# Output products of a fused attention and maxout kernel by Strassen's algorithm: seven block products for eight

## The chip, the cores and the metric

The kernel runs on one core of one Trainium2 chip. The metric is the device time of one execution in microseconds (us), the median of several runs. The engines are called as in the profile: PE (TensorE, matmuls; PEld is its weight load), DVE (VectorE), ACT (ScalarE), POOL (GpSimd) and SP (SyncE); a "q" behind a name means the engine's own instruction queue issuing a DMA.

## The reference

The first half is attention with blocks sorted by a soft permutation. `P` comes from five rounds of exp and row and column normalisation of `sort_net`. The second half is a feed-forward layer with a maximum of two hidden projections:

```python
k_sorted = np.einsum('bhij,bhjcd->bhicd', P, k_b)      # 8 blocks of 96 tokens
v_sorted = np.einsum('bhij,bhjcd->bhicd', P, v_b)
attn = softmax(scale * q_b @ k_sb.T)                   # inside each block
x = (attn @ v_sb)  ->  [B*S, H*D] = [3072, 512]
h1 = x @ w1                                            # w1, w2: [512, 1024]
h2 = x @ w2
g = np.maximum(h1, h2)
out = g @ w_out                                        # w_out: [1024, 512]
```

There are 4 batches of 8 heads, 768 tokens and 64 channels. Inputs and output are float32; the kernel computes its matmuls in bf16 with float32 accumulation.

## The kernel before

**The hidden layer.** max(h1, h2) is relu(h1 - h2) + h2, so the kernel keeps w1 - w2 in place of w1 (`w_difference`), computes one hidden product per token and takes its relu as `g`. What is left of h2 goes to the output through `wc` = w2 @ w_out, which `w_product` computes once. An output tile is therefore 12 matmuls with 128 rows of depth each: eight with `g` as the stationary operand and `wo_sb` moving, four with the attention output `xT` and `wc`.

**Tiles.** A batch of 768 tokens is cut into two halves `ch` of 384 (`TCH`) for the hidden layer. `moe_h(b, ch, t)` (lines 670 and 685) makes two of eight blocks of 128 hidden channels for one half in 8 matmuls of 384 columns, and ACT or DVE evicts them with the relu as a tile `g` of 128x768 bf16. The output is made in six token tiles `ti` of 128 tokens and 512 columns: `moe_out` (714) gives each tile 12 matmuls of 512 columns in two parts of six, two tiles share one PSUM tile of 1024 columns (two banks), and one copy evicts both, followed by one store of 512 KB from SP. Tiles 4 and 5 of the last batch go through `moe_out_last` (729), which evicts them one by one and splits the last tile into 384 and 128 columns.

**PSUM.** One pool of four buffers of 1024 float32 columns (line 62) serves everything. A new tile waits until the last reader of its buffer is done.

**Attention.** `sort_k` and the `sort_v` functions mix the blocks by P, `scores` (539) makes one unit of eight score blocks, ACT takes its exp into one of eight buffers `e` (line 555), `values` (567) multiplies by v and DVE evicts the result in two instructions, a reciprocal (586) and a scaled copy (592) into `x`. `x_transposes` (600) turns `x` into `xT`, by PE for batch 0 and by a DMA transpose on SP for the others. `turn_v` (line 250) reorders v on DVE, `pair_q` (407) packs q for batches 2 and 3, and `q_transposes` transposes it, by a DMA on SP in those batches.

**Order.** The schedule is written by hand: instructions stand on each engine in the order of the calls. The first part (about 38 us) loads, normalises P and does the attention and the hidden products of batch 0 by a list of steps. Then a loop over batches runs a list of units: eight `moe_h` (none in batch 0, which has four `w_product` instead), then twelve parts of output tiles. Behind a unit stand steps of the next batch's attention, as three tables (`first_tail`, `second_tail`, `third_tail`, lines 859 to 913) say; the last batch has none. So in batches 0 to 2 the output products alternate with sorts, scores and values of the next batch, and in batch 3 they follow one another. Which of ACT and DVE evicts a tile is decided at build time by `pick` (running sums of estimated work, `load`), or by a letter given.

**Queues.** Loads are issued by POOL, stores and DMA transposes by SP in the order of the calls.

Of the kernel before, what the change touches and what calls it, by code (L numbers as in the profile page):

```python
# [10 lines left out]
FP32 = mybir.dt.float32  # L11
# [5 lines left out]
def kernel(  # L17
# [16 lines left out]
    nc = tc.nc  # L34
# [18 lines left out]
    NE = 8  # L53
# [349 lines left out]
    def pair_q(b, two):  # L403

        if two == 0:
            q_pair[b] = qpool.tile([128, HP, R, 2 * D], BF16, tag="q_pair", name="q_pair", bufs=1)
        nc.vector.tensor_copy(
            out=q_pair[b][:, :, :, two * D : (two + 1) * D],
            in_=q_raw[b][:, two * HP : (two + 1) * HP].rearrange("p h (r d) -> p h r d", r=R),
        )  # L410
        load["D"] += 900
# [125 lines left out]
    e_tiles, x_tiles = {}, {}  # L537

    def scores(b, u, n=0):
# [15 lines left out]
        e = e_bufs[(b * 8 + u) % NE]  # L555
# [142 lines left out]
    out_ps = {}  # L698

    def out_products(dst, b, ti, n0=0, n1=512, part=None):  # L700
        ch, off = divmod(ti * 128, TCH)
        for m in range(NFB + HP) if part is None else range(part * 6, part * 6 + 6):
            hp = m - NFB
            nc.tensor.matmul(  # L704
                dst,
                g_tiles[b, ch, m // 2][:, m % 2, off : off + 128]
                if m < NFB
                else xT[:, b % 2, ch, hp % 2, hp // 2, off : off + 128],
                wo_sb[:, m, n0:n1] if m < NFB else wc[:, hp, n0:n1],
                start=(m == 0),  # L710
                stop=(m == NFB + HP - 1),
            )

    def moe_out(b, ti, part):
        slot = ti % 2
        if slot == 0 and part == 0:
            out_ps[0] = ps_f32("out_ps")
        ps = out_ps[0]
        out_products(ps[:, slot * 512 : (slot + 1) * 512], b, ti, part=part)
        if slot == 1 and part == 1:  # L720
            tok0 = b * S + ti * 128
            o = opool.tile([128, 2, 512], FP32, tag="o", name="o")
            evac(o.rearrange("p t n -> p (t n)"), ps, 1024)
            nc.sync.dma_start(
                out=out[tok0 - 128 : tok0 + 128, :].rearrange("(t p) n -> p t n", p=128),
                in_=o,
            )

    def moe_out_last(ti, pieces):

        tok0 = (B - 1) * S + ti * 128
        for n0, n1, eng in pieces:
            ps = ps_f32("out_ps")
            out_products(ps[:, 0 : n1 - n0], B - 1, ti, n0, n1)
            o = opool.tile([128, n1 - n0], FP32, tag=f"o{ti}{n0}", name="o", bufs=1)
            if eng == "A":
                nc.scalar.copy(out=o, in_=ps[:, 0 : n1 - n0])
            else:
                nc.vector.tensor_copy(out=o, in_=ps[:, 0 : n1 - n0])  # L739
            (nc.scalar if eng == "A" else nc.sync).dma_start(  # L740
                out=out[tok0 : tok0 + 128, n0:n1], in_=o
            )

# [107 lines left out]
    def sorts_and_scores(b):  # L851
# [6 lines left out]
    TURN = [lambda c=c: turn(both, c) for c in (0, 24, 48, 72)]  # L858
    first_tail = {
        7: KS,  # L860
        9: [TQ[0], TURN[0]],
        10: [SC[0], TQ[1], TURN[1]],
        11: SC[1:4] + TURN[2:4] + [lambda half=half: load_v(3, half=half) for half in range(2)],
        12: VS[0:3],
        13: VS[3:6],
        14: VS[6:8] + [SC[4]],
# [5 lines left out]
        20: [VA[4]],  # L872
        21: [VA[5], TR[2]],
        22: [VA[6], VA[7], TR[3]],
# [20 lines left out]
        17: [lambda: pair_q(3, 0)],  # L895
        18: [lambda: pair_q(3, 1)],
# [17 lines left out]
    tails = [first_tail, second_tail, third_tail, {}]  # L914
    for b in range(B):
# [52 lines left out]
```

## Time and profile before

| | us |
|---|---|
| median of the runs (165.81 to 166.31) | 165.84 |
| span of the profiled execution, first to last instruction | 165.0 |
| difference: what lies around the span | 0.84 |
| first output product of batch 0 | 49.8 |
| hidden products of batch 1, 2, 3 begin | 70.9, 104.1, 135.8 |
| output products of batch 1, 2, 3 begin | 84.9, 117.3, 146.2 |
| last output product begins its last four matmuls | 161.5 |

The profiled execution's own device time is not listed apart; its span and the median of the runs stand for it. The page gives each engine's busy time, a row of digits for 40 slices of the span, the chain of work that ended last, and groups of equal instructions with count, busy time, mean duration and the idle time ahead of them. A matmul's listed duration holds its way through the array (380 ns for 512 columns), while matmuls start every 216 ns; the distance between starts is what counts. In the answers on single stretches of time the first column is the start in us from the beginning of the span and the second the length.

### The profile page before, as it was taken

Reading aid. Unit: us, or ns where it says so; the run is one execution under the profiler, and the core shown is the slowest. Engines: PE = TensorE matmul, PEld = TensorE weight load, DVE = VectorE, ACT = ScalarE, POOL = GpSimd, SP = SyncE. Lnnn points to the kernel's source line nnn. Section 1 sums busy time; section 2 is a strip of 40 time slices with the busy share of each in tenths; the row PEclk is TensorE's granted clock in tenths of the full one; section 3 lists DMA queues with packets and bytes.
Section 4 is the critical chain, followed back from the end, with each engine's and each line's share of the span. In section 5 each row is a group of like instructions: output and inputs, shape, how many; then the busy total and the mean of one; then the engine's idle time right before and its main releaser. Section 6 shows DMA issues by size and latency. Waiting matters only on the chain.

```text
span 165.0 us, 4561 instructions
## 1 busy us (share of the span) xinstructions
PE 157.0 (95%) x2007; PEld 95.4 (58%) x2025; DVE 77.5 (47%) x170; ACT 82.3 (50%) x101; POOL 33.9 (21%) x61
## 2 busy tenths in 40 slices
PE   7889999999999999999999999999999999999992
PEld 7839776756554555557655554575655546654451
DVE  4878995684366564525277763250642420000011
ACT  3489776617239846055652353457447206642020
POOL 7949997131206000000014010000000000000000
PEclk9999999999999999999999999999999999999999
DMA  3999999999999999689515999995025294000333
GB/s 41 204 204 194 164 196 207 209 205 220 210 203 204 220 224 167 175 84 228 111 19 104 126 212 157 200 309 29 0 52 175 50 164 142 0 0 0 127 131 127
DMA packets 30404, 23.90 MB, mean 145 GB/s; under 512 B 16752, under 2 KB 25200, under 8 KB 30384
## 3 DMA queue, kind: packets, MB, share of 16 engines
q0 software_dynamic: 11040, 13.37, 50.0%
q1 hardware_dynamic: 19200, 10.17, 28.9%
q8 instruction: 16, 0.26, 0.7%
q10 hardware_dynamic: 144, 0.07, 0.1%
q14 instruction: 4, 0.03, 0.1%
HBM read 26.75 MB, written 6.29 MB: 200 GB/s over the span
## 4 chain that ended last, share of the span: by engine, by line
PE 81%; DMA 6%; DVE 5%; ACT 3%; POOL 2%; issue 2%
PE out_ps L704 37%; PE h_ps L677 25%; DMA w_sb<-in_moe_w_dram 5%; PE wc_ps L657 4%; PE o_ps L575 4%; PE k_ps L458 3%; PE s_ps L548 3%; ACT e L556 1%; POOL w_sb L189 1%; PE v_ps L523 1%; DMA p_sb<-in_sort_net_dram 1%; PE tq_ps L433 1%; DVE colsum L276 1%; DVE p_sb L273 1%; PE tw_ps L638 1%
## 5 line engine op out<-in xcount | busy, mean ns | idle before, releaser
L704 PE MATMUL out_ps<-wo_sb,g 128*128 128x512 bf16 (+2 forms) x187 | 46.0, 370 | 1.4 <-issue 1.0
L677 PE MATMUL h_ps<-xT,w_sb 128*128 128x384 bf16 x256 | 44.5, 326 | 0.0
L677 PEld LDWEIGHTS <-w_sb 128*128 128x128 bf16 x256 | 24.0, 98 | 15.5
L556 ACT ACTIVATE e<-s_ps 96x768 bf16<-96x768 f32 x32 | 24.0, 805 | 14.8 <-PE s_ps L548 14.8
L691 ACT ACTIVATE g<-h_ps 128x768 bf16<-128x768 f32 x27 | 21.7, 811 | 17.4 <-PE h_ps L677 17.3
L704 PEld LDWEIGHTS <-g 128*128 128x128 bf16 x200 | 17.1, 97 | 15.8
L704 PE MATMUL out_ps<-wc,xT 128*128 128x512 bf16 (+2 forms) x98 | 24.7, 370 | 0.1
L108 ACT COPY o<-out_ps 128x1024 f32<-128x1024 f32 x10 | 10.1, 1012 | 28.0 <-PE out_ps L704 25.2
L592 DVE TENSOR_TENSOR x<-o_ps,rs 96x512 bf16<-96x512 f32 x32 | 22.0, 687 | 1.1
L704 PEld LDWEIGHTS <-xT 128*128 128x128 bf16 x100 | 9.6, 97 | 11.2
L575 PEld LDWEIGHTS <-e 96*128 96x128 bf16 x256 | 11.7, 97 | 5.7 <-DVE v_sb L110 0.2
L586 DVE RECIPROCAL rs<-o_ps 96x8 f32<-96x8 f32 x32 | 6.4, 201 | 17.2 <-PE o_ps L575 17.1
L739 DVE COPY o<-out_ps 128x512 f32<-128x512 f32 (+1 forms) x2 | 1.2, 625 | 27.6 <-PE out_ps L704 27.6
L575 PE MATMUL o_ps<-v_sb,e 96*128 96x65 bf16 x256 | 12.7, 193 | 0.0
L110 DVE CAST kT<-k_ps 128x1024 bf16<-128x1024 f32 x6 | 7.2, 1222 | 8.4 <-PE k_ps L458 8.4
L110 DVE CAST v_sb<-v_ps 96x1024 bf16<-96x1024 f32 x7 | 8.5, 1219 | 4.9 <-PE v_ps L523 2.2
L160 POOL DMA_DIRECT2D v_raw<-in_k_dram x3 | 2.5, 838 | 35.1 <-DVE v_dc L250 31.4
L108 ACT CAST v_sb<-v_ps 96x1024 bf16<-96x1024 f32 x9 | 8.8, 1015 | 1.6 <-PE v_ps L500 0.8
L169 POOL DMA_DIRECT2D v_raw<-in_v_dram x11 | 6.5, 593 | 12.7 <-DVE v_dc L250 6.4
L693 DVE TENSOR_SCALAR g<-h_ps 128x768 bf16<-128x768 f32 x5 | 4.8, 957 | 8.9 <-PE h_ps L677 8.8
L548 PEld LDWEIGHTS <-kT 64*128 64x128 bf16 x256 | 6.1, 94 | 4.8 <-issue 2.6
L548 PE MATMUL s_ps<-qT,kT 64*128 64x96 bf16 x256 | 8.5, 204 | 0.3 <-DVE qT L110 0.2
(97 smaller groups left out, 144.4 us busy)
## 6 DMA issues: line engine op xcount, KB each, us to landing
out_dram<-o SPq DMA_DIRECT2D x11, 512.0 KB, 3.4
v_raw<-in_v_dram POOLq DMA_DIRECT2D x8, 384.0 KB, 13.5
k_raw<-in_k_dram POOLq DMA_DIRECT2D x9, 256.0 KB, 11.0
w_sb<-in_moe_w_dram POOLq DMA_DIRECT2D x4, 256.0 KB, 6.0
w_sb<-in_moe_w_dram POOLq DMA_DIRECT2D x2, 512.0 KB, 9.6
wo_sb<-in_moe_w_out_dram POOLq DMA_DIRECT2D x2, 512.0 KB, 13.7
v_raw<-in_v_dram POOLq DMA_DIRECT2D x3, 256.0 KB, 5.0
q_raw<-in_q_dram POOLq DMA_DIRECT2D x4, 192.0 KB, 9.1
```

The lines of the kernel that those rows point to most:

```text
L108: nc.scalar.copy(out=out_ap, in_=in_ap)
L110: nc.vector.tensor_copy(out=out_ap, in_=in_ap)
L169: nc.gpsimd.dma_start(out=v_raw[r0 : r0 + 64, m * n : (m + 1) * n], in_=v_src[b, :, m * n : (m + 1) * n],)
L548: nc.tensor.matmul(ps[:, h2 * 512 + ii * 128 : h2 * 512 + ii * 128 + BLK], kT[b][rows, (hp * 8 + i) * BLK : (hp * 8 + i) * BLK + 128], rhs ...
L556: nc.scalar.activation(out=e[:, 0 : 8 * BLK].rearrange("p (t c r) -> p t c r", t=8, r=R), in_=ps[0:BLK] .rearrange("p (t f) -> p t f", t=8 ...
L575: nc.tensor.matmul(ps[:, h2 * 512 + ii * 65 : h2 * 512 + (ii + 1) * 65], e[:, (h2 * 4 + ii) * BLK : (h2 * 4 + ii) * BLK + 128], v_sb[:, m0 ...
L586: nc.vector.reciprocal(out=rs, in_=ov[:, :, :, 64])
L592: nc.vector.tensor_tensor(out=x, in0=ov[:, :, :, 0:D], in1=rs.to_broadcast([BLK, 2, 4, D]), op=ALU.mult,)
L657: nc.tensor.matmul(ps[:, 0:512], w2T[:, fb, dmt * 128 : (dmt + 1) * 128], wo_sb[:, fb, :], start=(fb == 0), stop=(fb == NFB - 1),)
L677: nc.tensor.matmul(h_ps[ch, t][:, m * 512 : m * 512 + TCH], w1_sb[:, hp, fb * 128 : (fb + 1) * 128], xT[:, b % 2, ch, hp % 2, hp // 2, :], ...
L691: nc.scalar.activation(out=g, in_=src, func=AF.Relu)
L704: nc.tensor.matmul(dst, g_tiles[b, ch, m // 2][:, m % 2, off : off + 128] if m < NFB else xT[:, b % 2, ch, hp % 2, hp // 2, off : off + 12 ...
```

## The change

A batch's output is [768 tokens, 512 columns] = A @ B with a depth of 12 blocks of 128 (eight of `g`, four of `xT`). It is now cut in two along each of the three dimensions: token half `ch` 0 or 1, depth half, and column half of 256 (`NW`). The four block products of each output half, eight together, are replaced by seven products by Strassen's algorithm (in Winograd's form). A token tile of half 0 goes together with that of half 1; there are three such pairs in a batch, two handled as one group (`pair`, 12 matmuls of 256 columns a product) and one alone (`single`, six). A batch has 126 matmuls of 256 columns instead of 72 of 512.

- **Weight sums** (`weight_sums`): T1 to T4 of `wo_sb` and of `wc`, once, on DVE in the tail of batch 0. Six of them take the place of `w2T`, which is no longer needed then.
- **Token sums** (`x_sums`, `g_sums`): S1 to S4 of `xT` (four instructions of 128x768 bf16 a batch; on DVE for batch 0, on POOL for the others, behind the first hidden product) and of `g` (eight a batch, on DVE behind the last hidden product; S3 overwrites its operand).
- **Groups** (`Group.step`): seven products go by turns into the two banks of one PSUM tile; four of the seven accumulate on an earlier product that stays there. After each product one instruction evicts: an ACT copy after products 0 and 2, a DVE add of PSUM and an SBUF tile after the other five. Each group stores twice from SP, 512 KB for the pair and 256 KB for the single tile.
- **The last batch** uses the same groups; `moe_out_last` is gone.
- **Memory**: six `e` buffers instead of eight, and `q_pair` shares the buffer of `q_raw`.
- **Units**: twelve output parts become seven steps of the pair and four units of two, two, two and one steps of the single group; the tails are moved accordingly.

```diff
-    NE = 8
+    NE = 6
+    NW = DMODEL // 2
...
-            q_pair[b] = qpool.tile([128, HP, R, 2 * D], BF16, tag="q_pair", name="q_pair", bufs=1)
+            q_pair[b] = qpool.tile([128, HP, R, 2 * D], BF16, tag="q_raw", name="q_pair", bufs=1)
...
-        e = e_bufs[(b * 8 + u) % NE]
+        e = e_bufs[e_next[0] % NE]
+        e_next[0] += 1
...
-    def moe_out(b, ti, part):
-        slot = ti % 2
-        if slot == 0 and part == 0:
-            out_ps[0] = ps_f32("out_ps")
-        ps = out_ps[0]
-        out_products(ps[:, slot * 512 : (slot + 1) * 512], b, ti, part=part)
-        if slot == 1 and part == 1:
...
-            evac(o.rearrange("p t n -> p (t n)"), ps, 1024)
...
+    def weight_sums(c, which):
+
+        b11, b12, b21, b22 = weight_blocks(c)
+        t1, t3 = (wt_c[:, 0], wt_c[:, 2]) if c else (wt_early[:, 0], wt_early[:, 1])
+        t2, t4 = (wt_c[:, 1], wt_c[:, 3]) if c else (wt_late[:, 0], wt_late[:, 1])
+        out, in0, in1 = {
+            1: (t1, b12, b11),
+            2: (t2, b22, t1),
+            3: (t3, b22, b12),
+            4: (t4, b21, t2),
+        }[which]
+        nc.vector.tensor_tensor(out=out, in0=in0, in1=in1, op=ALU.subtract)
+        load["D"] += 330 if c else 600
+
+    def x_sums(b, which, eng):
+
+        a11, a12, a21, a22 = [xT[:, b % 2, ch, :, half, :] for ch in range(2) for half in range(2)]
+        s1, s2, s3, s4 = [sums_x[:, n] for n in range(4)]
+        out, in0, in1, op = {
+            1: (s1, a21, a22, ALU.add),
+            2: (s2, s1, a11, ALU.subtract),
+            3: (s3, a11, a21, ALU.subtract),
+            4: (s4, a12, s2, ALU.subtract),
+        }[which]
+        eng.tensor_tensor(out=out, in0=in0, in1=in1, op=op)
+
+    def g_sums(b, t):
+
+        a11, a12, a21, a22 = [g_tiles[b, ch, t + 2 * half] for ch in range(2) for half in range(2)]
+        s1, s2, s4 = [sums_g[:, n, t * 2 : t * 2 + 2] for n in range(3)]
+        for out, in0, in1, op in [
+            (s1, a21, a22, ALU.add),
+            (s2, s1, a11, ALU.subtract),
+            (s4, a12, s2, ALU.subtract),
+            (a21, a11, a21, ALU.subtract),
+        ]:
+            nc.vector.tensor_tensor(out=out, in0=in0, in1=in1, op=op)
+        load["D"] += 1900
...
+    class Group:
...
+        def product(self, bank, lw, rw, new):
+            n = 0
+            last = len(self.ks) * len(self.tiles) - 1
+            for k in self.ks:
+                for p, ti in enumerate(self.tiles):
+                    nc.tensor.matmul(
+                        self.ps[:, bank * 512 + p * NW : bank * 512 + (p + 1) * NW],
+                        left(self.b, lw, k, ti * 128),
+                        right(rw, k),
+                        start=new and n == 0,
+                        stop=n == last,
+                        skip_group_check=True,
+                    )
+                    n += 1
...
+        def add(self, ch, half, n, other):
+            nc.vector.tensor_tensor(
+                out=self.part(ch, half), in0=self.by_tile(self.bank(n)), in1=other, op=ALU.add
+            )
+            load["D"] += (60 + self.w) / 0.96
...
+        def step(self):
+            at, self.at = self.at, self.at + 1
+            if at == 0:
+                n = len(self.tiles)
+                self.ps = ps_f32("out_ps")
...
+                self.product(0, "a11", "b11", True)
+                nc.scalar.copy(out=self.a, in_=self.bank(0))
+                load["A"] += (200 + self.w) / 1.2
+            elif at == 1:
+                self.product(1, 2, 2, True)
+                self.add(1, 0, 1, self.by_tile(self.a))
+            elif at == 2:
+                self.product(0, "a12", "b21", False)
+                nc.scalar.copy(out=self.part(0, 0), in_=self.by_tile(self.bank(0)))
+                load["A"] += (200 + self.w) / 1.2
+            elif at == 3:
+                self.product(1, 1, 1, False)
+                self.add(0, 1, 1, self.by_tile(self.a))
+            elif at == 4:
+                self.product(0, 3, 3, True)
+                self.add(1, 1, 0, self.part(0, 1))
+            elif at == 5:
+                self.product(1, 4, "b22", False)
+                self.add(0, 1, 1, self.by_tile(self.a))
+                self.store(0)
             else:
+                self.product(0, "a22", 4, False)
+                self.add(1, 0, 0, self.part(1, 0))
+                self.store(1)
...
     first_tail = {
-        7: KS,
-        9: [TQ[0], TURN[0]],
-        10: [SC[0], TQ[1], TURN[1]],
-        11: SC[1:4] + TURN[2:4] + [lambda half=half: load_v(3, half=half) for half in range(2)],
+        7: KS + XS,
+        8: [GS[0]],
+        9: [TQ[0], TURN[0], WS[0, 1], WS[0, 3]],
+        10: [SC[0], TQ[1], TURN[1], GS[1]],
+        11: SC[1:4]
+        + TURN[2:4]
+        + [WS[0, 2], WS[1, 1], WS[1, 2]]
+        + [lambda half=half: load_v(3, half=half) for half in range(2)],
         12: VS[0:3],
         13: VS[3:6],
-        14: VS[6:8] + [SC[4]],
+        14: VS[6:8] + [SC[4], WS[1, 3], WS[0, 4], WS[1, 4]],
...
-        20: [VA[4]],
-        21: [VA[5], TR[2]],
-        22: [VA[6], VA[7], TR[3]],
+        20: [VA[4], VA[5], TR[2]],
+        21: [VA[6], VA[7], TR[3]],
...
+    def last_h(b):
+        moe_h(b, 1, 3, "A")
+        g_sums(b, 0)
+        g_sums(b, 1)
...
+        pair, single = Group(b, (0, 1), b > 0), Group(b, (2,), b > 0)
+        units += [pair.step] * 7
+        cost += [13] * 7
+        units += [lambda n=n: [single.step() for _ in range(n)] for n in (2, 2, 2, 1)]
+        cost += [13] * 4
         for n, unit in enumerate(units):
-            elapse(100 * cost[n] if n < len(cost) else 0)
+            elapse(100 * cost[n])
             unit()
+            if b > 0 and n == 0:
+                for which in (1, 2, 3, 4):
+                    x_sums(b, which, nc.gpsimd)
```

## The prediction

> **What bounds the kernel now.** I read the page's busy shares and slices first, then the chain by engine and line, the groups by shape for durations, the timeline of the last output tile, and the busy time by stage.
>
> ```profile
> PE 157.0 (95%) x2007; PEld 95.4 (58%) x2025; DVE 77.5 (47%) x170; ACT 82.3 (50%) x101; POOL 33.9 (21%) x61
> PE   7889999999999999999999999999999999999992
> PEclk9999999999999999999999999999999999999999
> PE 81%; DMA 6%; DVE 5%; ACT 3%; POOL 2%; issue 2%
> L704 PE MATMUL out_ps<-wo_sb,g 128*128 128x512 bf16 (+2 forms) x187 | 46.0, 370 | 1.4 <-issue 1.0
> ```
>
> TensorE is busy from 5 us to the end, holds 81% of the chain, and idles 1.4 us before the output products of line 704. Whatever makes it wait is paid in full. The last tile gives rates and latencies:
>
> ```profile
> 159.13 1.46 PE L704 MATMUL out_ps<-wo_sb,g 128*128 128x384 bf16 x8
> 159.34 0.69 DVE L739 COPY o<-out_ps 128x512 f32<-128x512 f32 x1 [26.31 <-PE out_ps L704]
> 160.43 0.81 PE L704 MATMUL out_ps<-wc,xT 128*128 128x384 bf16 x4
> 161.08 0.61 PE L704 MATMUL out_ps<-wo_sb,g 128*128 128x128 bf16 x8
> 161.53 0.39 PE L704 MATMUL out_ps<-wc,xT 128*128 128x128 bf16 x4
> ```
>
> Starts give the rate: eight 384-column matmuls take 160.43 - 159.13, 162 ns each; eight of 128 columns take 0.45 us, 56 ns each, a weight load apiece. So weight loads don't limit even there. Tile 4 left TensorE at 159.13 and its eviction began at 159.34: 0.21 us from the last matmul slot to an eviction.
>
> ```profile
> L739 DVE COPY o<-out_ps 128x512 f32<-128x512 f32 x1 | 0.7, 692 | 26.3 <-PE out_ps L704 26.3
> L330 DVE TENSOR_TENSOR pm<-pe,maskJ 128x320 f32<-128x320 f32 x1 | 0.5, 492 | 0.7 <-PE pe L322 0.7
> L108 ACT CAST wc<-wc_ps 128x512 bf16<-128x512 f32 x3 | 1.8, 586 | 5.8 <-PE wc_ps L657 5.8
> L737 ACT COPY o<-out_ps 128x128 f32<-128x128 f32 x1 | 0.3, 267 | 4.2 <-PE out_ps L704 4.2
> L231 DVE TENSOR_TENSOR w_sb<-w_sb 128x1024 bf16<-128x1024 bf16 x2 | 1.3, 688 | 0.3 <-DMA w_sb<-in_moe_w_dram 0.3
> L231 POOL TENSOR_TENSOR w_sb<-w_sb 128x1024 bf16<-128x1024 bf16 x2 | 4.3, 2146 | 0.4 <-DMA w_sb<-in_moe_w_dram 0.4
> ```
>
> These price the new operations. The busy time of the four output stages (batch 0 to 3) tells what lies beside them:
>
> ```profile
> 49.79:70.94 21.15, 20.49 (x291) 11.43 (x296) 12.47 (x23) 11.73 (x14) 2.18 (x4) 1.00 1.00 197
> 84.63:104.14 19.51, 18.98 (x222) 10.22 (x224) 12.63 (x21) 6.45 (x8) 3.07 (x4) 1.00 1.01 143
> 117.08:135.78 18.70, 18.48 (x174) 9.64 (x176) 6.68 (x15) 7.25 (x9) 0.00 (x0) 1.00 0.45 97
> 146.18:165.00 18.82, 15.63 (x84) 7.71 (x83) 1.25 (x2) 3.10 (x4) 0.00 (x0) 0.99 0.23 84
> ```
>
> Columns: window, length, then busy time of PE, weight load, DVE, ACT, POOL, clock, DMA share, GB/s. Batch 3 has almost nothing but products.
>
> **The change, part by part.** *Products.* A 512-column matmul takes 0.2158 us (the row of twelve from 148.77 to 151.36 in the timeline). With 56 ns at 128 columns, a straight line gives 109 ns at 256. Before: 276 of 512 columns, 12 of 384, 12 of 128, together 62.2 us. After: 4 batches of 126 matmuls of 256 columns, 504 x 0.1093 = 55.1. Gain 7.1 us, 1.8 a batch. A product of the pair group is 12 matmuls, 1.31 us; of the single group 6, 0.66.
>
> *The new wait.* A group's seven products alternate between the two banks of one PSUM tile, and each is evicted before the next but one uses its bank. By the source, one eviction would thus lie beside one product. The changed program's instruction list says otherwise: the first matmul of every product waits for the eviction of the product just before it, in the other bank. In batch 3 the matmul of product 2 (first bank) waits for the VectorE count that the add of product 1 (second bank) raises, product 3 for the ScalarE copy of product 2, and so on through all 48 boundaries (six in each of eight groups). The tile is tracked as a whole. So a boundary costs 0.21 + eviction + release, less what other work TensorE has between. Release: a VectorE cast of v_sb ends at 57.75 and the weight load waiting for it starts at 57.80; 0.06 is taken, 0.15 is the upper end, since that load's matmul started at 57.90.
>
> Evictions: add of 512 on VectorE 0.69 (the copy's row; 320 elements with a second operand take 492, on the same line), 256 by that line 0.42; ScalarE copy of 512 0.59, of 256 0.37 between 267 and 586. Boundaries: pair 0.86 (two, ScalarE) and 0.96 (four, VectorE), 5.6; single 0.64 and 0.69, 4.1. Uncovered 9.6 a batch, 38.6 in all. That is the price against a gain of 7.1.
>
> *VectorE's queue.* Operand sums of 128x768 bf16: 0.56 by the 688 row (0.155 fixed plus two elements a cycle), eight a batch, 4.3 us with neighbours overlapping 0.08 as two v_dc turns do; at one a cycle they would be 0.96, 3.2 us more a batch. Weight sums, once: 4 x 0.69 + 4 x 0.42 = 4.4. Batch 0 also forms four token sums, 2.0. They stand ahead of attention's evictions, turns and the new adds, which therefore start late.
>
> *Walk by stage, idle TensorE time added.* Batch 3 has no cover: 9.6, plus 0.4, since the add of product 1 stands behind the eight sums (4.05 us after the h products against 3.6). The tail grows: before, 161.75 to 165.0, 3.3; after 0.21 + 0.42 + 0.06, the 256 KB store (2.04 as for tile 4), and 1.0 to the end, 3.7. So 10.0 + 0.4 - 1.8 = +8.7.
> Batch 0: the last turns of v now follow token sums, four weight and hidden sums and end near 53.0 instead of 51.06; the v sorts behind product 0 wait, 1.9. Sorts and scores (0.7 to 1.1 us) cover the boundaries after products 1, 2. After 3: 1.1 (weight sums and a cast ahead of the add); 4: 0.7; 5: 0.4. Single group: 0.6, 0.4, 0.6, 0.2, 1.4 (two value units of 0.85 ahead of the add), 0.2. With 0.5 of switches, 8.1 - 1.8 = +6.3.
> Batch 1: 0.6; then 2.8, because the add of product 1 waits behind eight sums, two value evictions and a turn, to 6.0 us after the h products; 0.1 (scores cover); 0.7, 0.7, 0.7 (a value unit covers 0.24). Single: 0.8, 0.5, 0.6, 0, 1.0 (a cast ahead), 0.7. Switches 0.5: +8.0.
> Batch 2: 1.1 (the third score tile after product 0 waits for the exp of the first, whose PSUM buffer it takes), 1.3 (sums ahead of the add), 0.6, 0.7, 0.3, 0.7; single 0.6, 0.7, 0.6, 0.5, 0.7, 0.7: 8.6 - 1.8 = +6.8.
>
> *The rest.* ScalarE's copies stand ahead of few exps; counted above. GpSimd's four token sums (1.6 each by the 2146 row) run inside the h products, 13 us, and are first needed at product 1; without that cover, up to 6.4 a batch. The next k loads on its queue come after them, when their buffer is free. SyncE issues 16 stores at 0.37 instead of 13; in batch 1 the last store and x transpose reach the queue 0.45 later against the h products, and the q transpose behind them landed 0.13 us before its use: 0.3. Six exp buffers for eight and the shared q buffer cost nothing: each is reused over 1 us after its reader; were that gone, an exp, 0.8.
>
> *Sum.* 8.7 + 6.3 + 8.0 + 6.8 + 0.3 = 30.1 on the profiled span of 165.0, 195.1; the runs' median, 165.84, lies 0.84 above that span: 196.0.
>
> **Rivals.** *The clock falls.* All slices show clock 9, but the longest TensorE gap before was 1.1 us, once at 7.3; walked here, some 40% of batch 3's stage is idle in gaps of 0.7 to 1 us. If the clock halved in that stage alone, its 13.8 us of products would double: 209.8. No row shows it; for it speaks only how regular the gaps are. [...]
>
> *The waits are hidden* (other side). If a boundary were free because the banks alternate, the sum is -7.1, +1.9 for the late turns, +0.4 tail, +0.4 for single products shorter than their eviction: 161.4, or up to 2.8 more where VectorE's 20.5 us of queue in batch 1 exceeds TensorE's 17.7. It decides if the 48 boundaries average under 0.15 us; the instruction list speaks against it.
>
> *Attention covers batches 0 to 2.* Only batch 3 pays (8.7), the others gain 5.4 and lose 1.9: 171.0. Against: a value unit covers 0.24 of 0.96 and puts 0.85 ahead of the add.
>
> **Numbers.** Serialised, 0.84; clock 0.08; attention covers 0.05; hidden 0.03. Predicted 196.0. Its ends: release 0.15 on some 40 open boundaries +3.6; sums at one element a cycle, +3 a batch where they lead, partly counted, +8; below, covers better than walked, -8. Range 187 to 207, holding nearly all of the first case. About 0.3% is what a measurement here tells from no change. Faster 0.03, same 0.01, slower 0.96.
>
> **What would show it.** Right: idle time before the matmuls of the out_ps tile, ended by VectorE and ScalarE evictions of that tile, about 30 us or more; matmul starts 109 ns apart; in batch 3 a regular rhythm of 1.3 us products and 0.9 us gaps; GpSimd never named by a TensorE wait. Wrong: evictions overlapping products of the other bank, a slice of the clock row under 9, sums of 0.96, or starts over 109 ns apart.

## The result, and the profile after

The changed kernel takes 197.2 us (median of five runs, 196.0 to 197.7), the kernel before 165.9 (165.8 to 166.3): 1.187 times as long, with a 95% interval of 1.184 to 1.191. Forecast were 196.0 us and a range of 187 to 207. The profiled execution took 196.0 us, of which the span is 193.8.

First the page of the kernel after: span, busy time of TensorE, its 40 slices and the granted clock.

```profile
span 193.8 us, 5110 instructions
...
PE 159.3 (82%) x2229; PEld 118.3 (61%) x2229; DVE 117.9 (61%) x247; ACT 80.6 (42%) x108; POOL 53.4 (28%) x73
...
PE   7999999999696877999477778997777699866661
...
PEclk9999999999999999999999999999999999999999
```

TensorE was busy in 95% of the span before and is now in 82%. The dents lie in four places, the four output stages; the clock row is flat, so time is lost between instructions and not in slower ones. (The other four executions had a mean granted clock of 0.986 to 0.991 and spans of 194.9 to 195.9; falls of the clock that traces show stand further down.)

The waits of TensorE, longest in total first: who waited, for whom, microseconds in total, how often, the longest.

```profile
PE out_ps L789 <- DVE o L809: 19.4, 28, 2.5
PE out_ps L789 <- ACT a L834: 3.4, 6, 0.8
PE out_ps L789 <- ACT o L841: 2.9, 6, 0.7
PE v_ps L524 <- DVE v_dc L251: 1.4, 1, 1.4
```

No wait of an output product for an eviction stood in this list before. Now 40 of them (28, 6 and 6) cost 25.7 us, all for an eviction of `out_ps` itself, and they make up most of the 28.8 us by which the span grew. Batch 3, which has nothing beside its products, shows the rhythm. In this timeline the first column is the start, the second the length, and the bracket holds the idle time before and what ended it.

```profile
175.29 0.60 PE L789 MATMUL out_ps<-w2T,sums_x 128*128 128x256 bf16 x4 [0.84 <-DVE o L809]
175.72 1.04 PE L789 MATMUL out_ps<-wt_early,g 128*128 128x256 bf16 x8
177.54 0.60 PE L789 MATMUL out_ps<-wc,sums_x 128*128 128x256 bf16 x4 [0.78 <-DVE o L809]
...
187.81 0.38 PE L789 MATMUL out_ps<-wc,sums_x 128*128 128x256 bf16 x2 [0.52 <-DVE o L809]
...
189.14 0.38 PE L789 MATMUL out_ps<-w2T,xT 128*128 128x256 bf16 x2 [0.51 <-DVE o L809]
```

A pair's product recurs every 177.54 - 175.29 = 2.25 us, of which 12 x 0.109 = 1.31 are matmuls: a boundary (the time from one product's last matmul to the next product's first) of 0.94. A single tile's product recurs every 189.14 - 187.81 = 1.33, of which 0.66 are matmuls: 0.67. The four output stages, batch 0 to 3 (window, length, busy time of PE, weight load, DVE, ACT, POOL, then clock, DMA share, GB/s):

```profile
49.54:75.98 26.44, 20.64 (x350) 17.10 (x350) 20.16 (x39) 11.61 (x16) 1.61 (x4) 1.00 0.76 160
89.94:117.44 27.50, 19.48 (x280) 16.07 (x279) 19.37 (x36) 7.88 (x12) 4.04 (x5) 1.00 0.86 125
130.38:155.70 25.32, 18.74 (x232) 15.34 (x230) 15.29 (x32) 7.04 (x11) 0.00 (x0) 1.00 0.29 74
166.10:193.80 27.70, 15.85 (x127) 12.07 (x125) 9.43 (x18) 2.73 (x5) 0.00 (x0) 1.00 0.15 57
```

The stages sum to 106.96 us against 78.18 before; between them only the hidden products of batch 1 grew, by 0.27. (In batches 1 and 2 these windows, before and after alike, begin 0.25 us ahead of the first output product, with a unit of eight value matmuls of attention.) VectorE is the engine with the most new work (77.5 to 117.9 us), yet in every stage it has idle time left, 6 us or more. Two theories fit this table so far: the products wait because the tile is tracked as a whole (a product that writes one bank waits for the eviction of the other), or they wait because VectorE, with sums and adds in one queue, is late. The experiments separate them.

### The profile page after: what moved, and what is told of

The parts are those of the page before. It is cut to its first block, busy times and chain, and to the rows that moved or that the text cites. A ratio compares the mean times of both kernels' runs of the same rounds, so it can differ in the third digit from the quotient of the medians.

```text
span 193.8 us, 5110 instructions
## 1 busy us (share of the span) xinstructions
PE 159.3 (82%) x2229; PEld 118.3 (61%) x2229; DVE 117.9 (61%) x247; ACT 80.6 (42%) x108; POOL 53.4 (28%) x73
## 5 line engine op out<-in xcount | busy, mean ns | idle before, releaser
L738 POOL TENSOR_TENSOR sums_x<-xT 128x768 bf16<-128x768 bf16 x6 | 10.1, 1688 | 70.9 <-DMA xT<-x 70.9
L809 DVE TENSOR_TENSOR o<-out_ps,a 128x512 f32<-128x512 f32 (+1 forms) x24 | 13.3, 555 | 26.5 <-PE out_ps L789 20.2
L789 PEld LDWEIGHTS <-sums_x 128*128 128x128 bf16 x96 | 9.2, 97 | 16.1 <-issue 14.9
L789 PE MATMUL out_ps<-w2T,sums_x 128*128 128x256 bf16 x72 | 11.7, 271 | 8.8 <-DVE o L809 3.3
L789 PEld LDWEIGHTS <-sums_g 128*128 128x128 bf16 x144 | 13.8, 97 | 5.1 <-issue 3.3
L809 DVE TENSOR_TENSOR o<-out_ps,o 128x512 f32<-128x512 f32 (+1 forms) x16 | 8.9, 555 | 9.9 <-PE out_ps L789 9.8
L789 PE MATMUL out_ps<-wo_sb,g 128*128 128x256 bf16 x96 | 13.1, 272 | 0.4 <-DVE o L809 0.3
L841 ACT COPY o<-out_ps 128x512 f32<-128x512 f32 (+1 forms) x8 | 3.8, 479 | 22.3 <-PE out_ps L789 22.2
L789 PE MATMUL out_ps<-wc,xT 128*128 128x256 bf16 x48 | 7.8, 271 | 6.1 <-DVE o L809 6.0
L577 PEld LDWEIGHTS <-e 96*128 96x128 bf16 x256 | 11.6, 97 | 1.6
L750 DVE TENSOR_TENSOR sums_g<-g 128x768 bf16<-128x768 bf16 x8 | 4.4, 552 | 9.5 <-ACT g L693 9.5
```

The lines of the kernel that those rows point to most:

```text
L577: nc.tensor.matmul(ps[:, h2 * 512 + ii * 65 : h2 * 512 + (ii + 1) * 65], e[:, (h2 * 4 + ii) * BLK : (h2 * 4 + ii) * BLK + 128], v_sb[:, m0 ...
L738: eng.tensor_tensor(out=out, in0=in0, in1=in1, op=op)
L789: nc.tensor.matmul(self.ps[:, bank * 512 + p * NW : bank * 512 + (p + 1) * NW], left(self.b, lw, k, ti * 128), right(rw, k), start=new and ...
L809: nc.vector.tensor_tensor(out=self.part(ch, half), in0=self.by_tile(self.bank(n)), in1=other, op=ALU.add)
L841: nc.scalar.copy(out=self.part(0, 0), in_=self.by_tile(self.bank(0)))
```

## The experiments

In what follows "stage" is the time from a batch's first output product to the next batch's first hidden product (or to the end), "front" all that lies before the weight product `w_product` of batch 0, which started at 39.97 before. Counted like this, batches 1 and 2 start 0.25 us later than in the windows above: the stages sum to 77.68 us in the kernel before and 106.48 in the changed one, and the hidden products of batches 1 and 2 take 13.94 and 13.19 us before, 14.20 and 13.18 after.

### One PSUM tile for each bank

```diff
-    psum = ctx.enter_context(tc.tile_pool(name="psum", bufs=4, space=bass.MemoryType.PSUM))
+    psum = ctx.enter_context(tc.tile_pool(name="psum", bufs=3, space=bass.MemoryType.PSUM))
+    acc = ctx.enter_context(tc.tile_pool(name="acc", bufs=1, space=bass.MemoryType.PSUM))
...
-                self.ps = ps_f32("out_ps")
+                first = 0 if n == 2 else 1
+                self.ps = [
+                    acc.tile([128, 512], FP32, tag=f"acc{(i + first) % 2}", name="out_ps")
+                    for i in range(2)
+                ]
```

> The two banks of a group become two PSUM tiles of their own (a second pool of two 512-column tiles; the first pool drops from four to three tiles to make room). Products, sums, evictions and their order stay. Theory (the tile is tracked as a whole, so each product waits for the eviction before it): the first matmul of a product no longer waits for the eviction of the other bank; a pair product of 1.31 us covers an eviction of 0.86 to 0.96, a single one of 0.66 covers 0.64 to 0.69 all but 0.03. The 25.7 us that the out_ps tile's matmuls wait for evictions go, but for what the sums hold up in batches 0 and 1 (1.4 and about 1.5) and what three attention tiles instead of four cost: 161 to 168 us, batch 3's stage 27.7 -> 18 to 18.5. Rival (VectorE's queue, with the sums ahead of the evictions, is the bound in batches 0 to 2): only batch 3 recovers, at most 9.6: 187 or more.

Measured: 176.3 us (175.5 to 177.0), 1.058 times the kernel before (1.053 to 1.063), 20.9 under the changed kernel. Batch 3 in the timeline of this run:

```profile
161.69 0.60 PE L790 MATMUL out_ps<-w2T,sums_x 128*128 128x256 bf16 x4
161.90 0.69 DVE L810 TENSOR_TENSOR o<-out_ps,a 128x512 f32<-128x512 f32 x1 [1.66 <-PE out_ps L790]
162.13 1.04 PE L790 MATMUL out_ps<-wt_early,g 128*128 128x256 bf16 x8
163.00 0.60 PE L790 MATMUL out_ps<-wc,sums_x 128*128 128x256 bf16 x4
163.26 0.69 DVE L810 TENSOR_TENSOR o<-out_ps,o 128x512 f32<-128x512 f32 x1 [0.67 <-PE out_ps L790]
```

Products start 1.31 us apart without a gap, and the add of one bank (161.90 to 162.59) runs while the other bank is written. The output stages of the run:

```profile
56.14:77.74 21.60, 19.71 (x355) 16.83 (x352) 19.18 (x39) 11.33 (x16) 1.55 (x3) 1.00 0.72 140
93.66:112.87 19.21, 18.05 (x276) 15.41 (x273) 17.70 (x34) 7.41 (x11) 2.89 (x3) 1.00 0.95 112
126.92:145.15 18.23, 17.13 (x228) 14.73 (x225) 14.87 (x32) 7.03 (x11) 0.00 (x0) 1.00 0.35 91
155.55:174.70 19.15, 14.41 (x128) 12.13 (x125) 9.44 (x18) 2.72 (x5) 0.00 (x0) 1.00 0.23 83
```

With nearly the same VectorE work in each stage (19.18 against 20.16 us, 17.70 against 19.37, and so on) the stages fall from 106.48 to 78.19 us, 28.3 of the 28.8 that the change had cost them. VectorE's queue is therefore not what most of this time was lost to, and the rival, which put 187 us or more, falls. But the total was missed by 8: the front became 6.1 longer (the weight product starts at 46.05) and the hidden products of batches 1 and 2 took 15.92 and 14.05 us instead of 13.94 and 13.19. Nor did the stages fall below those of before, though 7.1 us of matmuls are gone. Both remainders are taken up below.

### The kernel before with three PSUM tiles

```diff
-    psum = ctx.enter_context(tc.tile_pool(name="psum", bufs=4, space=bass.MemoryType.PSUM))
+    psum = ctx.enter_context(tc.tile_pool(name="psum", bufs=3, space=bass.MemoryType.PSUM))
```

> The kernel before with three PSUM tiles instead of four: what giving a fourth of PSUM to the products' own tiles costs by itself, to be subtracted from the run with split banks. Both theories: 166 to 168 us; TensorE would wait for an exp, a cast or a product's eviction one tile sooner.

Measured: 182.5 us, 1.097 times the kernel before (1.092 to 1.101). The expectation was far off. The front alone loses 5.0 us (weight product at 45.00), so most of the front's loss with split banks is the missing tile. The other 1 us arose in the split's execution between 26 and 29 us, while its clock stood at 0.50 (shown at the end): a transpose group that both runs have starts at 27.75 here and at 29.00 there, though the matmuls just before that stretch start within 0.15 us of each other. The hidden products of batches 1 and 2 take 15.24 and 14.38 us with three tiles, 2.5 more than with four. The stages here are not comparable to those of the split, since the output products share the three tiles:

```profile
55.51:80.45 24.94, 21.02 (x291) 11.66 (x296) 11.21 (x22) 11.42 (x13) 1.55 (x3) 1.00 0.64 128
```

Batch 0 needs 24.94 us instead of 21.15. One PSUM tile of four is worth 16 us to this kernel, as much as half of what the change cost.

### No operand sums, with one tile and with two

These two kernels leave the sums out, so their output is not the reference's; they serve for their times alone.

```diff
-        nc.vector.tensor_tensor(out=out, in0=in0, in1=in1, op=ALU.subtract)
...
-        eng.tensor_tensor(out=out, in0=in0, in1=in1, op=op)
+        return
...
     def left(b, which, k, off):
+        which = "a22" if which in (1, 2, 3, 4) else which
...
     def right(which, k):
+        which = "b22" if which in (1, 2, 3, 4) else which
```

> The changed kernel without any operand sum: the four token sums, eight hidden sums a batch and eight weight sums are left out, and the products that read them read a plain block instead; same number and shape of matmuls, same evictions, one PSUM tile for both banks (the output is no longer the reference's). Theory: the serialised boundaries stay, only what the sums held up goes: 1.4 (late turn of v in batch 0), 1.5 (the 2.51 us wait of product 1 in batch 1, down to the 0.96 of a boundary), 0.4 in batch 3, about 0.4 in batch 2: 197.2 - 3.8 = 193.4 us (191 to 195.5). Rival (VectorE's queue): some 22 us of VectorE work go, and with them most of the loss: 180 us or less.

> Both: split banks and no operand sums (the output is no longer the reference's). Theory: the floor of the idea with its matmuls and evictions alone, below the run with split banks by the 1 to 4 us that sums hold up there: 160 to 164 us. Rival (VectorE's queue): this is the only one of the three that comes near 160; split banks alone stay above 187.

Measured: with one tile 190.4 us, 6.8 under the changed kernel; with split banks 170.7, 5.6 under the split with sums, and 6.7 above the upper end of what was expected, since the missing tile costs as much here (the weight product starts at 44.84). The stages of the first (one tile, no sums):

```profile
49.43:74.21 24.78, 20.73 (x350) 17.25 (x350) 15.75 (x29) 11.52 (x16) 2.39 (x4) 1.00 0.82 171
88.55:113.53 24.98, 19.24 (x277) 15.83 (x273) 16.18 (x30) 7.64 (x12) 1.95 (x3) 1.00 0.85 138
126.71:150.37 23.66, 18.38 (x228) 15.12 (x225) 11.13 (x24) 7.03 (x11) 0.00 (x0) 1.00 0.31 79
160.77:188.30 27.53, 15.85 (x128) 12.14 (x125) 5.58 (x10) 2.72 (x5) 0.00 (x0) 0.96 0.16 58
```

Taking 3.2 to 4.4 us of VectorE work out of each stage gives back 1.66, 2.28, 1.42 and 0.17 us of it. (The clock of 0.96 in batch 3 comes from the last of the 40 slices of the page's clock row, 183.6 to 188.3, the only one under 9; the last matmul ends there at 184.4.) In batch 3 VectorE's work falls by 41% and the stage by 0.6%. So sums have a price where attention's evictions stand behind them: 5.5 us in the stages, where 3.8 was expected, and as much between the spans of the two profiled executions (193.8 and 188.3). The 6.8 between the medians holds 1.3 more, nearly all of it because the profiled execution of the changed kernel was its shortest.

With split banks the stages sum to 73.48 us without sums and 78.19 with them. The four runs together part the two causes:

| stages, us | with sums | without |
|---|---|---|
| one tile for both banks | 106.48 | 100.95 |
| a tile for each bank | 78.19 | 73.48 |

The shared tile costs 28.3 us with the sums and 27.5 without them, the sums 5.5 with one tile and 4.7 with two. Those 4.7 us are where most of the 7.1 us of saved matmuls goes even with the waits removed. What takes the rest was followed in batch 3 alone: 13.77 us of matmuls, 0.73 waiting for a hidden sum, 0.6 in small gaps of the single tiles, 4.05 from the last matmul to the end against 3.3 before.

### Pools exchanged at each stage, and the order of the sums

The split again, but the PSUM pools are closed and reopened at both ends of every output stage, so that three tiles serve only the stages themselves. The second run also changes the order of the sums and stores half of the last tile early.

```diff
+    def split_psum(out, n=[0]):
+        nonlocal psum, acc
+        n[0] += 1
+        pools.close()
+        psum = pools.enter_context(
+            tc.tile_pool(name=f"psum{n[0]}", bufs=3 if out else 4, space=bass.MemoryType.PSUM)
+        )
...
+            if unit == pair.step and pair.at == 0:
+                split_psum(True)
+            if b > 0 and n == 0:
+                split_psum(False)
```

```diff
-        g_sums(b, 0)
-        g_sums(b, 1)
+        for part in (slice(0, 2), slice(2, 4)):
+            g_sums(b, 0, part)
+            g_sums(b, 1, part)
...
+                if self.last:
+                    self.store(1, slice(NW, DMODEL))
...
-                self.store(1)
+                self.store(1, slice(0, NW if self.last else DMODEL))
```

> Split banks again, but the PSUM pools are closed and opened anew: four tiles wherever no output products run (the front and the hidden products of batches 1 to 3), three tiles and the two bank tiles only from a batch's first output product to its last. Theory (what the run with split banks still lost, 176.3 against 166.3, is the missing fourth tile in the front and in the hidden products, not the products): front and hidden products as in the kernel before (49.8, 13.9, 13.2, 10.4), output stages as in the run with split banks (21.6, 19.2, 18.2, 19.15): span 165.5, 167 to 169 us. Rival (the front lost its 6 us to something else the change moves, such as six exp buffers or the clock that fell to 0.50 there): 174 us or more.

> As the run before it, and two things more: the hidden sums that product 1 reads are formed before the other four (the 0.73 us that product 1 waited for a hidden sum in batch 3 should go, and as much at most in batches 1 and 2), and the last tile's first output half is stored as soon as it is final, so that only 128 KB are left for the end. Theory: 0.7 to 1.5 us less for the order, 0.3 to 0.6 for the store: 1 to 2 us under the run before it, 165.5 to 167.5 us. Rival (VectorE's queue as a whole, not the order in it, holds product 1 up): under 0.6 us less.

Measured: 1.103 times the kernel before (1.098 to 1.108) and 1.108 times (1.102 to 1.114), where 167 to 169 us and 1 to 2 us less had been expected. The executions took 182.8 to 187.0 us and 182.7 to 185.7. The front is back (weight product at 39.19 in the first run), and so are the hidden products of batches 1 and 2 once the idle time at their end is taken off (13.89 and 13.35 us): both had been longer for want of the fourth tile. But the total is worse. TensorE of the first of the two:

```profile
92.84 1.01 PE L804 MATMUL out_ps<-wc,xT 128*128 128x256 bf16 x4 [4.16 <-DVE x L609]
...
132.34 1.01 PE L804 MATMUL out_ps<-wc,xT 128*128 128x256 bf16 x4 [5.26 <-DVE x L609]
```

The first product of a stage waits 4 to 5 us for a VectorE instruction of attention whose result it does not read. That instruction reads `o_ps`, a PSUM tile of the closed pool, and stands behind the eight hidden sums in VectorE's queue. So it looks as if the new pool's tiles are given out only when the old one's last user is done, while the schedule has attention running across that point; this is argued from the wait and the source, and no run tests it apart. With 2.16 us ahead of batch 0's first output product these waits make 11.6 us, and the matmuls behind them ran at a clock of 0.50 for 3.4 us or more each time (last section). The two runs scatter by 3 to 4 us and say nothing of the order of the sums.

```diff
     load.update(A=600.0, D=300.0)
+    front_psum.close()
+    psum = ctx.enter_context(tc.tile_pool(name="psum_out", bufs=3, space=bass.MemoryType.PSUM))
+    acc = ctx.enter_context(tc.tile_pool(name="acc", bufs=1, space=bass.MemoryType.PSUM))
```

> Split banks as in the first run of that name, but the pool of four tiles serves the whole front and is exchanged once, before the weight product of batch 0, for three tiles and the two bank tiles. Theory: the front as in the kernel before (the weight product starts near 39.5 instead of 46.05), one emptying of the pool of 1.8 to 2.5, and from the first output product on the lengths of the run with split banks (118.5): 176.3 - 6.5 + 2 = 171.8, 170.5 to 173 us. Rival (the new pools cost the time wherever they are opened, or the front's loss was the clock at 0.50): 175 us or more.

Measured: 171.65 us, 1.031 times the kernel before (1.027 to 1.035), as expected. One exchange, at the end of the front, keeps four tiles where they were worth 5 us and pays the emptying once (weight product at 41.06, 1.1 later than before). The hidden products of batches 1 and 2 still take 16.40 and 14.05 us, 3.3 over before, with three tiles. That accounts for the distance of 5.2 between the two spans: 1.4 before the first output product, 3.3 in the hidden products, 0.5 in the output stages (78.20 against 77.68).

### Batch 3 alone, with two tiles and with one

In batch 3 no attention needs PSUM, so the groups can take two of the four ordinary tiles. Batches 0 to 2 go back to `moe_out`; the weight sums run on VectorE beside the hidden products of batch 3. The order of the sums and the early store are kept.

```diff
-                self.ps = ps_f32("out_ps")
+                self.ps = [ps_f32("out_ps") for _ in range(2)]
...
+        if b < B - 1:
+            units += [
+                lambda ti=ti, part=part: moe_out(b, ti, part)
+                for ti in range(6)
+                for part in range(2)
+            ]
+        else:
+            units[7] = lambda: last_h(b)
+            pair, single = Group(b, (0, 1)), Group(b, (2,))
+            units += [pair.step] * 7 + [single.step] * 7
```

> Seven products for eight in batch 3 alone, with one PSUM tile for each bank out of the pool of four, the weight sums on VectorE and the token sums on GpSimd beside the hidden products of batch 3, and the order and the early store of the run before it; batches 0 to 2 form their output products as the kernel before does. Theory: the stage of batch 3 takes 13.8 us of products, some 0.2 of gaps and a tail of 3.8, 17.8 to 18.2 against 18.82, and nothing else moves: 0.6 to 1.0 us under the kernel before. Rival (the sums in front of the hidden layer's evictions, or two output buffers instead of three, cost as much again): within 0.3% of the kernel before or above it.

The control differs from it in three lines, which put both banks into one tile again:

```diff
-                        self.ps[bank][:, p * NW : (p + 1) * NW],
+                        self.ps[:, bank * 512 + p * NW : bank * 512 + (p + 1) * NW],
-            return self.ps[n][:, 0 : self.w]
+            return self.ps[:, n * 512 : n * 512 + self.w]
-                self.ps = [ps_f32("out_ps") for _ in range(2)]
+                self.ps = ps_f32("out_ps")
```

> The kernel with seven products in batch 3 alone, with one thing turned back: the two banks of a group lie in one PSUM tile again instead of two. Same matmuls, sums, evictions, order and queues. Theory (the tile is tracked as a whole): the twelve boundaries of batch 3 are paid again, 2 x 0.86 + 4 x 0.96 + 4.1 = 9.6, less the few tenths that the two-tile version had in gaps: 165.45 + 8.7 to 9.6 = 174.2 to 175.1 us. Rival (TensorE waited for VectorE and ScalarE as such, and the two tiles helped only by leaving attention's tiles alone): there is no attention in batch 3, so 166 us or less.

Measured: with two tiles 165.45 us (eleven runs, 165.1 to 166.3) against 166.32 for the kernel before, a ratio of 0.994 (0.993 to 0.996); with one tile 174.1 us, 1.048 (1.044 to 1.053). The first is as expected, the second 0.1 under. Two products of the version with two tiles, then the same two of the version with one:

```profile
153.72 0.60 PE L821 MATMUL out_ps<-wc,sums_x 128*128 128x256 bf16 x4
154.16 1.04 PE L821 MATMUL out_ps<-wo_sb,sums_g 128*128 128x256 bf16 x8
155.03 0.60 PE L821 MATMUL out_ps<-w2T,xT 128*128 128x256 bf16 x4
```

```profile
158.09 0.60 PE L821 MATMUL out_ps<-wc,sums_x 128*128 128x256 bf16 x4 [0.78 <-DVE o L841]
158.52 1.04 PE L821 MATMUL out_ps<-wo_sb,sums_g 128*128 128x256 bf16 x8
160.34 0.60 PE L821 MATMUL out_ps<-w2T,xT 128*128 128x256 bf16 x4 [0.78 <-DVE o L841]
```

Only the tiles differ: a product every 1.31 us or every 2.25. Batch 3's stage is 18.11 us with two tiles, 26.94 with one, 18.82 in the kernel before:

```profile
146.39:164.50 18.11, 14.32 (x127) 12.11 (x125) 9.33 (x18) 2.72 (x5) 0.00 (x0) 1.00 0.24 88
```

```profile
146.66:173.60 26.94, 15.84 (x127) 12.15 (x125) 9.34 (x18) 2.73 (x5) 0.00 (x0) 0.98 0.16 59
```

This is the theory's claim by itself: the same matmuls, the same VectorE work (9.33 and 9.34 us), and 8.83 us between the two stages, 8.65 between the medians. (The clock of 0.98 comes from the last slice of the page's clock row, 169.3 to 173.6, the only one under 9; the last matmul ends there at 170.5.) The version with two tiles is also the only one that beats the kernel before, by about 0.9 us, half a per cent: 1.76 of matmuls saved in batch 3, of which 0.55 are lost to one wait of the fourth product for an add that stands behind the other sums, some 0.4 to small gaps, and 0.1 to the tail (3.4 from the last matmul to the end, against 3.3).

## Why the prediction was right

The time came out 1.2 us above the forecast, and the stages (the windows of the first section) bear out the walk, not only its sum. (Some of its sums are rounded up: the 48 boundaries at the prices named come to 38.4 us and not 38.6, the terms of batches 0 and 2 to 8.0 and 8.5 and not 8.1 and 8.6. Nothing hangs on that.)

| | before | after | difference | forecast |
|---|---|---|---|---|
| first output product at | 49.79 | 49.54 | -0.25 | 0 |
| stage of batch 0 | 21.15 | 26.44 | +5.3 | +6.3 |
| stage of batch 1 | 19.51 | 27.50 | +8.0 | +8.0 |
| stage of batch 2 | 18.70 | 25.32 | +6.6 | +6.8 |
| stage of batch 3 | 18.82 | 27.70 | +8.9 | +8.7 |
| hidden products, batches 1 to 3 | 37.03 | 37.30 | +0.27 | +0.3 |
| span | 165.0 | 193.8 | +28.8 | +30.1 |
| around the profiled span | | 2.2 | | 0.84 |

**The matmuls.** Right. Starts are 109 ns apart where nothing waits (12 in 1.31 us), which gives the 7.1 us saved.

**The new wait.** Right, and the step that carries the result. It came from reading which semaphore each product waits for, against what the source suggests by giving the two banks different names. The control in batch 3 shows it by itself. Its price, 0.21 + eviction + release, was good to 0.05 us: in batch 3 a pair's boundary was forecast at 0.86 behind ScalarE and is 0.84 and 0.89, at 0.96 behind VectorE and is 0.94 to 1.00, but 1.22 for the one add that stands behind the sums; a single tile's was forecast at 0.64 and 0.69 and is 0.61 to 0.67 and 0.67 to 0.73. The twelve come to 9.9 us, where 9.6 and 0.4 for that add had been forecast.

**The new instructions.** Right, by rows of the kernel after: the sums take 0.56, not the 0.96 that the upper end of the range allowed for, GpSimd's 1.69, the adds 0.69. (The forecast's "cycle" is the 1.05 ns that one more element adds to the f32 copies of the kernel before: 558 ns for 384, 692 for 512.)

```profile
L809 DVE TENSOR_TENSOR o<-out_ps,a 128x512 f32<-128x512 f32 x12 | 8.2, 686 | 11.5 <-PE out_ps L789 5.1 <-issue 3.8 <-ACT e L558 2.5
L750 DVE TENSOR_TENSOR sums_g<-sums_g,g 128x768 bf16<-128x768 bf16 x8 | 4.5, 558 | 0.3
L738 POOL TENSOR_TENSOR sums_x<-xT 128x768 bf16<-128x768 bf16 x6 | 10.1, 1688 | 70.9 <-DMA xT<-x 70.9
```

GpSimd appears in no wait of TensorE in that trace, as forecast.

**VectorE's queue.** Right in place, not quite in size. The late turn of v in batch 0 was put at 1.9 us and the add of product 1 in batch 1 at 2.8; they cost 1.40 and 2.51:

```profile
52.41 0.88 PE L524 MATMUL v_ps<-bd,v_dc 64*128 64x64 bf16 x48 [1.40 <-DVE v_dc L251]
...
96.55 0.60 PE L789 MATMUL out_ps<-wc,xT 128*128 128x256 bf16 x4 [2.51 <-DVE o L809]
```

The turn is half of what batch 0 was overestimated by; which boundaries were better covered there than walked stays open. On the other hand the stages gained 5.5 us without the sums where I expected 3.8 from those two and smaller terms, so some of what the walk booked as plain boundaries in batches 0 to 2 were, it seems, boundaries with an add queued behind sums. The total hid that.

**The queue on SyncE.** Right, with its mechanism. The 0.3 us put down for a q transpose that lands late in batch 1 is one wait of the trace, where the kernel before has none:

```profile
84.78 0.52 PE L549 MATMUL s_ps<-qT,kT 64*128 64x96 bf16 x16 [0.39 <-DMA qT<-q_pair]
```

**Around the span.** Wrong by 1.4 us. I took 0.84 as the difference between the runs' median and the profiled span, which need not belong to one execution. Paired execution by execution, the kernel before has 1.7 to 1.9 (a span of 164.4 in a run of 166.14, for one) and the one after 1.8 to 2.2, the profiled one 2.2. This error and the 1.3 us by which the span was overestimated, batch 0 above all, cancelled: that the profiled execution took the forecast's 196.0 us to the tenth was luck. The median execution's 197.2 is a span of 195.2, at a mean clock of 0.986, and 2.0 around it.

**What was to be seen.** The out_ps waits came to 25.7 us, less than the "about 30 or more" of the text: part of the loss stands in waits of other tiles, such as the 1.4 for v and 1.0 of a score unit for an exp.

**The rivals.** That the waits are hidden, or that attention covers them in batches 0 to 2, is refuted by the stage table: these three lose 19.9 us together. That the clock falls in batch 3 did not happen in the profiled execution: 1.00 in a stage in which TensorE is busy for 57% of the time and idles 12 times for 0.46 to 1.05 us between products. The halving of the clock in this stage, from which this rival's 209.8 was worked out, is shown by no run; the falls to 0.50 that other runs show are told in the last section.

## What to carry to other kernels

Two banks in one PSUM tile acted as one buffer here (in batch 3 a pair's product every 2.25 us, and every 1.31 with a tile for each bank): before counting on an eviction beside the next product, look at what the next product's first matmul waits for, and give each bank a tile of its own if they are to overlap. A saving in matmul work of 7 us is soon spent if every product needs its own eviction: with the waits gone, the operand sums took 4.7 of it and the tile that the split needed took more (about 5 in the front and 3 in the hidden products). So trade only where PSUM and VectorE have little else to do: here it paid in the last batch alone.

## What was unexpected of the hardware

**The clock fell at three long waits of TensorE, and not in batch 3's short gaps.** In the run with pools exchanged at each stage, TensorE idled 2.16, 4.16 and 5.26 us ahead of the first three output stages, and the matmuls after each ran at a clock of 0.50: the four from 92.84 and the four from 132.34 took 0.81 us to the next start, the four from 97.59, behind such a stretch, 0.44. The windows around the three idles (the column before the DMA share is the granted clock):

```profile
48.49:51.90 3.41, 1.25 (x30) 1.11 (x25) 3.34 (x7) 2.58 (x4) 0.52 (x1) 1.00 1.21 204
51.90:55.31 3.41, 3.41 (x60) 2.48 (x58) 2.41 (x4) 2.10 (x3) 1.55 (x3) 0.50 1.27 220
88.70:92.80 4.10, 0.00 (x0) 0.00 (x0) 3.88 (x8) 0.83 (x2) 0.00 (x0) 1.00 0.42 64
92.80:95.80 3.00, 2.96 (x20) 2.24 (x21) 0.00 (x0) 0.16 (x1) 0.00 (x0) 0.51 0.76 51
127.00:132.30 5.30, 0.08 (x3) 0.00 (x0) 5.03 (x11) 0.69 (x1) 0.00 (x0) 0.82 0.00 0
132.30:136.90 4.60, 4.56 (x41) 3.17 (x42) 0.00 (x0) 1.76 (x3) 0.00 (x0) 0.50 0.24 43
```

By the first two lines the clock went from 1.00 to 0.50 at 51.90, after 3.41 us in which TensorE was busy for 37% (1.25 us). The second fall came as the 4.16 us of idle time ended, the third within the 5.26 us (mean clock 0.82). The mean clocks of other windows of this trace (0.72 from 92 to 94 us, 0.93 from 96 to 98, 0.60 from 130 to 132, 0.69 from 136 to 138) give an estimate of the two later stretches at 0.50, if it is 1.00 on either side of them: 92.9 to 96.3 and 130.4 to 137.2, so 3.4 and 6.8 us. In batch 3 of the changed kernel 12 gaps of 0.46 to 1.05 us in 24 us of products leave the clock at 1.00 (TensorE is busy for 15.85 of the 23.90 us from 166.10 to 190.00), and so does the wait of 2.51 us in its batch 1 (94.04 to 96.55; 1.00 in it and in the 3.45 us after it). So the length of one wait does not decide by itself, since a fall followed 2.16 us and none 2.51; what does was not shown.

Nor does every fall stand behind a long wait. With split banks the clock went to 0.50 for about 3.4 us (25.86 to 29.28, worked out in the same way from 0.86 in 25.5 to 26 and 0.72 in 29 to 29.5), after nine microseconds in which TensorE was busy for 75% and no gap was longer than 0.61:

```profile
17.00:26.00 9.00, 6.76 (x155) 5.11 (x151) 6.96 (x13) 5.85 (x8) 8.83 (x10) 0.99 1.27 184
26.00:29.20 3.20, 3.14 (x23) 2.50 (x24) 1.94 (x3) 0.38 (x1) 1.93 (x3) 0.50 1.24 206
```

From 23 to 26 us TensorE is busy for 2.14 of 3.00 us, 71%, nearly all with matmuls of 65 to 96 columns. Two other executions of the same kernel had a mean clock of 1.00 and spans 1.1 and 1.4 us shorter, and the kernel before with three tiles has the same gaps there and no fall (9 in all 40 slices of its clock row). Why it falls in one execution and not in the next was not settled. The spread of the changed kernel's own spans is of the same size, but only the shortest of its executions has a trace.

**Two VectorE copies took 3.5 times as long beside GpSimd's sums.** The copies that pack q took 547 to 556 ns each before. In the changed kernel the pair that met GpSimd's token sums took 1956 each, the other pair 546:

```profile
116.65 3.83 DVE L408 COPY q_pair<-v_raw 128x1536 bf16<-128x1536 bf16 x2
```

```profile
116.52 1.63 POOL L738 TENSOR_TENSOR sums_x<-xT 128x768 bf16<-128x768 bf16 x1 [12.44 <-DMA xT<-x]
118.23 1.83 POOL L738 TENSOR_TENSOR sums_x<-sums_x,xT 128x768 bf16<-128x768 bf16 x1
```

The first copy is issued at 116.65, GpSimd's sum ends at 118.15, and the 1.50 us between them and 0.55 for the copy itself make 2.05, near the 1956 ns. In the run without sums the two take 552 each. So it looks as if a copy waits for the sum that runs beside it; this is read from these times alone, and no run tests it apart. It cost 2.8 us of VectorE time; what of it reached TensorE was not measured.
